# Staged weights, whole-slot splits, a rebuilt routing turn and a transposed large part in a two-layer mixture-of-experts kernel

## The chip, the cores and the metric

One NeuronCore of a Trainium2 chip runs the whole kernel in one launch. Its engines take their instructions in order, each from its own list: the tensor engine (PE, with its weight loads shown apart as PEld), the vector engine (DVE), the scalar engine (ACT), GpSimd (POOL) and SyncE (SP, which here only issues DMAs). The metric is the device time of one execution in microseconds (us), lower is better.

## The reference, cut to what matters

Three stages in a chain, on two batches of 576 tokens (1152 in all), width 512:

```python
# 1: linear attention, 8 heads a batch
q_p, k_p = phi(q), phi(k)             # [exp(p), exp(-p)] of p = x @ w_phi less its largest magnitude
out = (q_p @ (k_p.T @ v)) / (q_p @ k_p.sum() + 1e-6)
# 2: first mixture: every expert on every token, gates P made doubly stochastic in 8 rounds
for e in range(8):
    out += P[:, e:e+1] * (np.maximum(x @ w1[e], 0) @ w2[e])      # 512 -> 1024 -> 512
# 3: second mixture: each token at one expert, at most cap = 288 tokens each
logits = x @ w_gate; expert = argmax(logits); gate = softmax(logits)[expert]
pos = place of the token among those of its expert, in order of tokens
h = np.maximum(disp[e, pos] @ w1[e], 0); y = h @ w2[e]           # own weights, 8 experts
out[token] = gate * y    if pos < cap else 0
```

## The kernel before

All products are fp32 in effect: each operand is split as x = hi + lo, two numbers that PE takes at full rate, and a product is hi*hi + hi*lo + lo*hi.

The first mixture runs in 36 units (an expert's 256 features each); the tokens go in two groups. A unit's weights come by two DMAs of 512 KB (`r<-w1a`, `r<-w2a`, `Unit`, L190), ACT makes hi and POOL lo (`split1`, `split2`); layer 1 (L617 to 619) is seven products of blocks in place of eight, layer 2 (L670 to 672) goes to PSUM, and DVE adds it with its gate to `acc` (L681). Attention of the eight head pairs is interleaved with the first units by the framework's scheduler; the scheduler also places those DMAs in SP's list.

The turn between the mixtures is written by hand from `by_hand` (after L828) on. `Route` (L690) takes some of the nine tiles of 128 tokens through steps: `turn` transposes a tile of `acc`, `logits` multiplies by w_gate and takes the largest and its index, `pick` makes the one-hot `oh` and running counts `ohs`, `place` counts the tokens before each token of its expert (`cp`, in PSUM), `slots` makes the slot number, `gate` the gate, `scatter` writes rows with an indirect DMA to their slots in memory (`disp`). Tiles 0 to 3 (A) go early, 4 and 5 (B) next, 6 to 8 (C) last. For experts 0 and 1 the transposed rows of the first 64 slots are made on PE instead (`xst`): a product of the last five tiles with the selection matrix `sel` (L925), and of the rows that were scattered before with the identity (L931). `pair_split` makes hi and lo of them, and expert 0 begins.

The second mixture loops over the experts (L1205 on). The first 64 slots of an expert take the small path: `q1_small` (16 matmuls of 512 columns, hi and lo of x side by side), `gt_small` copies to SBUF, `ht_small` adds both halves and transposes, `relu_small` makes `hhl` (ACT the relu, DVE the lo, L1123), `q2_small` (16 matmuls), `out_small` adds the halves with the gate and writes rows with an indirect DMA. Slots 64 to 287 take `large`, under a branch on whether the expert has so many tokens; in the profiled execution experts 2 and 6 do. Each expert has 8 pieces of weights of 128x1024 (4 of w1b, 4 of w2b), loaded by SP into 4 KB slots (`load`), and split by `Splits`: ACT makes hi but of piece 4, which DVE makes; lo goes half a slot at a time (128x512, L571), of five pieces on DVE, of three on POOL, into another slot. The loop says which steps of the next expert stand where in the engines' lists.

Of the kernel before, what the change touches and what calls it, by code (L numbers as in the profile page):

```python
# [20 lines left out]
def tile_linear_attention_two_moe(  # L21
# [27 lines left out]
    # the first layer's tokens in groups, each of two halves  # L49
# [7 lines left out]
    # tiles of a batch's tokens; the last, a half, is of both heads of a pair, one above the other  # L57
# [43 lines left out]
    )  # L101
    twice = const.tile([P, 64], F32, name="twice")
# [29 lines left out]
    rings = {"a": ring, "b": ring, "x": ring}  # L132
# [14 lines left out]
    # x and its sums (A11, A21 + A22, .. of the seven products), hi and lo, by group and half of the chunks of a block  # L147
# [10 lines left out]
    # the first group's are in slots: the blocks that are made in pairs, and the single ones  # L158
# [31 lines left out]
    class Unit:  # L190
        """an expert's weights for FQ of its features: chunk 2 i + k of W1 is in half k of the rows"""
# [48 lines left out]
    def a_parts(i, key):  # L240
        """the first keys' first columns come by themselves"""
# [18 lines left out]
    def phi_group(hl, g, d, nm):  # L260
        """x w_phi - max|x w_phi| for one or two tiles of rows, both heads of the pair"""
# [101 lines left out]
    def a_xtrans(i, c):  # L363
# [8 lines left out]
        if len(full) < len(TGS[c]):  # L372
            # of a half tile's block, each head's rows have their own columns
# [23 lines left out]
    def x_sums(g, c):  # L397
        """the seven products' left sides; chunk 2 i + k of x is in half k of the columns"""
# [31 lines left out]
    lgs = {}  # L430
    # of each token: its expert, logits, logits less the largest, expert as a number, slot
# [3 lines left out]
    def gate_logits(g):  # L435
        """x w_gate; of the second half S1 = A21 + A22 by the first rows of w_gate, and A22 by what the others are more"""
# [49 lines left out]
    def zero_fill(what):  # L486
        """empty slots and zero rows, from a part of acc that nothing needs yet"""
# [17 lines left out]
    def take(key, shape, dt, name):  # L505
        """the slot that has been free for the longest"""
        at[key] = free.pop(0)
        return slot_at(at[key], shape, dt, name)

    def load(n, keep):  # L510
        """weights of the second layer's experts, in order: n pieces, but leave the slots for hi of keep's"""
        while n and todo:
            e, i = todo[0]
            if len(free) <= sum(x[0] <= keep and x not in sp.h for x in raws) + (e <= keep) + sp.more:
                break
            del todo[0]
            w, cc, W = (w1b, DC // 4, F) if i < 4 else (w2b, F // P // 4, D)
            raws[e, i] = take(("r", e, i), [P, cc, W], F32, f"rw_{e}_{i}")
            r0 = i % 4 * cc * P
            nc.sync.dma_start(raws[e, i], w[e, r0 : r0 + cc * P, :].rearrange("(c p) f -> p c f", p=P))  # L520
            n -= 1

    class Splits:
        """hi and lo of the second layer's weights, half a slot at a time; each engine takes its share in order"""

        WHOLE = "a"
        HI_V, LO_P, LO_P0, LATE = (4,), (0, 3, 5), (1, 2, 5), (4, 6, 7)

        def __init__(self):
            self.q = {k: [] for k in "avp"}  # L530
            self.spare, self.more = {k: [] for k in "vp"}, 2
            self.h, self.l, self.hi_todo, self.lo_todo = {}, {}, {}, {}
            for e in range(E):
                for i in range(8):
                    for k in range(2):
                        he = "v" if e and i in self.HI_V else "a"
                        le = "p" if i in (self.LO_P if e else self.LO_P0) else "v"
                        self.q[he].append(("hi", e, i, k))
                        self.q[le].append(("lo", e, i, k))
                        self.hi_todo[e, i, k], self.lo_todo[e, i, k] = he, le  # L540

        def emit(self, eng, most=2):
            what, e, i, k = self.q[eng].pop(0)
            r = raws[e, i]
            if (e, i) not in self.h:
                shape, nm = list(r.shape), f"h2_{e}_{i}"
                self.h[e, i] = take(("h", e, i), shape, R32, nm)
            n = 1
# [761 lines left out]
```

## Time and profile before

| | us |
|---|---|
| median of 3 runs (lowest, highest) | 1082.06 (1081.43, 1083.75) |
| profiled execution, span from first to last instruction | 1079.5 |
| PE busy | 1037.5 (96%) |
| DVE busy | 749.9 (69%) |
| POOL busy | 526.6 (49%) |
| ACT busy | 401.6 (37%) |
| HBM read, written | 84.25 MB, 11.51 MB |

Busy shares are means over the whole span; attention and the first mixture fill the first 894 us, the turn and the second mixture the rest, and these have different limits. The profile's views give: busy shares in 40 slices, groups of instructions by line and tile, the waits of an engine with what ended them, and the instructions in order of time.

### The profile page before, as it was taken

To read this page: it belongs to the slowest core of one execution; us is meant where nothing else is said; L and a number is where in the kernel's file an instruction comes from. 1 tells how busy PE (TensorE), PEld (TensorE's weight loads), DVE (VectorE), ACT (ScalarE), POOL (GpSimd) and SP (SyncE) were. 2 spreads that over 40 slices of the span, in tenths; PEclk is the share of its full clock that TensorE was granted. 3 is DMA by queue.
4 is the path that set the end of the run, shared out by engine and by line. 5 is a ranking of instruction groups with operands and counts; after the bars stand their busy time and mean duration, and the time that the engine had idled before them with its cause. 6 is when DMAs were issued, how large, how long until landed. Compare 5 with 4: busy or idle time off the path is not lost. (4 is left out here: it accounts for less than half of the span.)

```text
span 1079.5 us, 16720 instructions
## 1 busy us (share of the span) xinstructions
PE 1037.5 (96%) x6214; PEld 926.3 (86%) x6214; DVE 749.9 (69%) x1400; ACT 401.6 (37%) x841; POOL 526.6 (49%) x524
## 2 busy tenths in 40 slices
PE   7999999999999999999999999999999998798787
PEld 7999989898899899889988988898899888576566
DVE  6755799996666666666666666666667667946962
ACT  5767543322223222222232232223222235717532
POOL 4656897644454554444455544444542016625631
PEclk9999999999999999999999999999999998989889
DMA  8813132211112111111111111111111433967700
GB/s 272 273 53 89 62 98 79 79 59 40 39 40 59 49 51 39 39 40 39 46 53 59 40 40 40 39 41 59 58 57 63 131 110 104 323 229 239 264 7 25
DMA packets 56024, 95.21 MB, mean 88 GB/s; under 512 B 6206, under 2 KB 25022, under 8 KB 55936
## 3 DMA queue, kind: packets, MB, share of 16 engines
q1 hardware_dynamic: 54544, 91.41, 26.4%
q0 software_dynamic: 1392, 2.63, 0.7%
q8 instruction: 55, 0.90, 0.4%
q14 instruction: 33, 0.27, 0.1%
HBM read 84.25 MB, written 11.51 MB: 89 GB/s over the span
## 5 line engine op out<-in xcount | busy, mean ns | idle before, releaser
L81 POOL TENSOR_TENSOR l<-r,h 128x256 fp32r<-128x256 f32 (+2 forms) x100 | 154.2, 1555 | 351.4 <-ACT h L80 351.4
L681 DVE SCALAR_TENSOR_TENSOR acc<-p,prob,acc 128x512 f32<-128x512 f32 x252 | 188.3, 749 | 105.2 <-PE p L672 105.1
L670 PE MATMUL p<-h,hh 128*128 128x512 f32 x576 | 228.4, 396 | 0.0
L671 PE MATMUL p<-l,hh 128*128 128x512 f32 x576 | 227.4, 395 | 0.0
L672 PE MATMUL p<-h,hl 128*128 128x512 f32 x576 | 227.3, 395 | 0.0
L636 DVE TENSOR_TENSOR ca<-ca,p 128x256 f32<-128x256 f32 (+1 forms) x256 | 112.6, 449 | 70.2 <-PE p L619 68.0
L80 ACT CAST h<-r 128x256 fp32r<-128x256 f32 (+2 forms) x108 | 70.9, 686 | 184.8 <-PE p L672 163.6
L625 ACT ACTIVATE hh<-ca 128x320 fp32r<-128x320 f32 (+1 forms) x128 | 56.2, 442 | 217.9 <-DVE ca L636 217.9
L672 PEld LDWEIGHTS p<-h,hl 128*128 128x128 f32 x576 | 108.4, 188 | 25.6
L670 PEld LDWEIGHTS p<-h,hh 128*128 128x128 f32 x576 | 108.4, 188 | 22.4
L671 PEld LDWEIGHTS p<-l,hh 128*128 128x128 f32 x576 | 108.4, 188 | 22.3
L81 POOL TENSOR_TENSOR lt<-t,ht 128x256 fp32r<-128x256 f32 x144 | 124.9, 896 | 1.3 <-PE pn L349 1.3
L571 DVE TENSOR_TENSOR l<-rw,h 128x512 fp32r<-128x512 f32 x80 | 82.8, 1066 | 15.2 <-ACT h L558 13.3
L571 POOL TENSOR_TENSOR l<-rw,h 128x512 fp32r<-128x512 f32 x48 | 69.7, 1474 | 30.1 <-ACT h L558 23.2
L617 PE MATMUL p<-xh,ht 128*128 128x320 f32 x256 | 79.2, 309 | 0.0
L619 PE MATMUL p<-xh,lt 128*128 128x320 f32 x256 | 79.1, 309 | 0.0
L618 PE MATMUL p<-xl,ht 128*128 128x320 f32 x256 | 79.1, 309 | 0.0
L617 PE MATMUL p<-xs,ht 128*128 128x256 f32 x256 | 72.9, 285 | 0.7 <-DVE cb L636 0.5
L619 PE MATMUL p<-xs,lt 128*128 128x256 f32 x256 | 72.6, 284 | 0.0
L618 PE MATMUL p<-xs,ht 128*128 128x256 f32 x256 | 72.4, 283 | 0.0
L636 DVE TENSOR_TENSOR cb<-cb,p 128x320 f32<-128x320 f32 (+1 forms) x128 | 58.0, 453 | 19.0 <-PE p L619 18.0
L629 DVE SCALAR_TENSOR_TENSOR hl<-ca,hh 128x320 fp32r<-128x320 f32 (+1 forms) x128 | 65.7, 515 | 2.5 <-ACT hh L625 2.0
(253 smaller groups left out, 2296.6 us busy)
## 6 DMA issues: line engine op xcount, KB each, us to landing
r<-w1a SPq DMA_DIRECT2D x36, 512.0 KB, 3.5
r<-w2a SPq DMA_DIRECT2D x36, 512.0 KB, 3.8
rw<-w1b SPq DMA_DIRECT2D x32, 512.0 KB, 6.1
rw<-w2b SPq DMA_DIRECT2D x32, 512.0 KB, 8.4
disp<-acc SPq DMA_DIRECT2D x18, 260.0 KB, 4.9
v<-va SPq DMA_DIRECT2D x8, 325.0 KB, 3.7
rawq<-qT SPq DMA_DIRECT2D x8, 320.0 KB, 4.7
out<-acc SPq DMA_DIRECT2D x9, 256.0 KB, 5.5
```

Source lines behind the costliest of these rows:

```text
L80: nc.scalar.copy(hi, src)
L81: (eng or nc.vector).tensor_tensor(lo, src, hi, ALU.subtract)
L571: en.tensor_tensor(self.l[e, i].rearrange("p c f -> p (c f)")[:, ks], rv, hv, ALU.subtract)
L617: nc.tensor.matmul(ps, ws_[0], xs[0], start=i == 0, stop=False)
L618: nc.tensor.matmul(ps, ws_[0], xs[1], start=False, stop=False)
L619: nc.tensor.matmul(ps, ws_[1], xs[0], start=False, stop=i == DI - 1)
L629: nc.vector.scalar_tensor_tensor(lv[:, qs], src, 0.0, hv[:, qs], ALU.max, ALU.subtract)
L636: nc.vector.tensor_tensor(o, x, ps, ALU.add)
L670: nc.tensor.matmul(ps, a, w.w2[0][:, f, :], start=f == 0, stop=False)
L671: nc.tensor.matmul(ps, a, w.w2[1][:, f, :], start=False, stop=False)
L672: nc.tensor.matmul(ps, b_, w.w2[0][:, f, :], start=False, stop=f == FT - 1)
L681: nc.vector.scalar_tensor_tensor(o, ps, prob[:, t, e : e + 1], o, ALU.mult, ALU.add)
```

## The change

- `stage`: after each layer 2 of a unit two pieces of the second mixture's weights are copied in memory, from w1b and w2b to `wst`, where a piece is 128 rows of 4 KB; `load` reads `wst`. Three more slots "f" and one more "e".
- `Splits`: ACT makes all hi, lo is made in whole slots in the place of the raw weights: expert 0's on POOL during the last units, all others on DVE.
- `Route`: B is tiles 4 and 5, C 6 and 7, Z 8; `place` adds -4096 in PSUM where a token is at an expert, and `select` compares `cp` with numbers that carry the same mark; slots and gates of tiles 4 to 8 are made together (R); exponentials come from PSUM with the largest as bias; one scatter of five tiles at the end.
- The loop: lo of the next expert's pieces and all hi at new places; the rest of the steps inside the branch, between the features of `large`, or in its other arm; loads eight before and four after the slots come free.
- `large`: weights are the stationary side, 224 tokens the moving one; h comes out transposed.
- `dynamic_dma_scratch_size=4096`.

```diff
+    def stage(n):
+        for e, i in staged[:n]:
+            src = piece(e, i)
+            nc.sync.dma_start(wst[e, i].rearrange("p (c f) -> p c f", c=src.shape[1]), src)
+        del staged[:n]
...
-            nc.sync.dma_start(raws[e, i], w[e, r0 : r0 + cc * P, :].rearrange("(c p) f -> p c f", p=P))
+            nc.sync.dma_start(raws[e, i], wst[e, i].rearrange("p (c f) -> p c f", c=src.shape[1]))
...
-        HI_V, LO_P, LO_P0, LATE = (4,), (0, 3, 5), (1, 2, 5), (4, 6, 7)
+                    le = "v" if e else "p"
+            h, l = self.h[n], r.bitcast(R32)
+            self.put(eng, lambda: en.tensor_tensor(l, r, h, ALU.subtract))
...
+        def aside(self, hi, lo):
+            steps = {k: [] for k in "avp"}
+            self.put, put = (lambda eng, f: steps[eng].append(f)), self.put
+            self.run("v", -1, lo)
+            self.run("a", -1, hi)
...
+                todo = before[::-1] + [(tri_b, oh[:, t, :]), (far_b, oh[:, t, :])]
...
+        def select(self, iota_s):
+                nc.vector.tensor_tensor(
+                    sel[:, j], iota_s, self.cp[:, j * E : j * E + EP].unsqueeze(2).to_broadcast([P, EP, C0]), ALU.is_equal
+                )
...
                 if pend:
                     yield from layer2(*pend)
+                    stage(2)
...
+                        sp.run("p", 6, (0, 7))
...
-        A, B, C = (Route(range(*r)) for r in ((0, 4), (4, 6), (6, NT)))
+        A, B, C, Z = (Route(range(*r)) for r in ((0, 4), (4, NT - 3), (NT - 3, NT - 1), (NT - 1, NT)))
+        R = Route(range(4, NT))
...
+        Z.place()
+        Z.exps(0)
+        sp.run("a", 4, (1, 7))
+        C.select(iota_s)
+        Z.select(iota_s)
...
+        R.slots()
+        R.gate()
+        rows_of([xs0], [ident])
+        rows_of([acc[:, Z.t0]], [Z.sel[:, 0]], last=True)
+        xhl = pair_split(0, xqp, xst)
+        R.scatter()
...
+        def q1(f):
+            for c in range(DC):
+                nc.tensor.matmul(ps, w1[0][c][:, fs], xh[:, c], start=c == 0, stop=False)
+                nc.tensor.matmul(ps, w1[0][c][:, fs], xl[:, c], start=False, stop=False)
+                nc.tensor.matmul(ps, w1[1][c][:, fs], xh[:, c], start=False, stop=c == DC - 1)
+            nc.scalar.activation(hh, ps, AF.Relu)
+            nc.vector.scalar_tensor_tensor(hl, ps, 0.0, hh, ALU.max, ALU.subtract)
+            for k in "av":
+                if aside[k]:
+                    aside[k].pop(0)()
+        def q2(f):
+            for i, (_, n) in enumerate(chunks):
+                nc.tensor.matmul(o, hh[:, ts], w2[0][f], start=f == 0, stop=False)
+                nc.tensor.matmul(o, hh[:, ts], w2[1][f], start=False, stop=False)
+                nc.tensor.matmul(o, hl[:, ts], w2[0][f], start=False, stop=f == F // P - 1)
...
-        sp.run("a", 2, nx)
+        sp.run("v", 8, (e + 1, AHEAD - 1))
...
+        sp.run("a", 8, (e + 1, AHEAD + 1))
...
+        aside = sp.aside((e + 2, AHEAD + 1), (e + 2, AHEAD - 1))
...
+            with more.Else():
+                for f in aside["a"] + aside["v"]:
+                    f()
+        load(8, E)
         sp.done(e)
-        load(4, e + 2)
+        load(4, E)
```

DVE's list where expert 3's small path stands, from the branch of expert 2 to the output of expert 2. `rw` is a raw piece, `h` its hi, `l` its lo, `hhl` the relu's lo, `y` the output. Before:

```order
L1245 UNCONDITIONAL_BRANCH x2
L558 CAST h_3_4_10684<-rw_4_10083 128x512
L571 TENSOR_TENSOR l_3_4_10686<-rw_4_10083,h_3_4_10684 128x512
L558 CAST h_3_4_10684<-rw_4_10083 128x512
L571 TENSOR_TENSOR l_3_4_10686<-rw_4_10083,h_3_4_10684 128x512
L571 TENSOR_TENSOR l_3_6_10692<-rw_6_10087,h_3_6_10690 128x512 x2
L571 TENSOR_TENSOR l_3_7_10697<-rw_7_10089,h_3_7_10695 128x512 x2
L1123 SCALAR_TENSOR_TENSOR hhl_0_10756<-ht_0_10751,hhl_0_10756 128x4x64
L1123 SCALAR_TENSOR_TENSOR hhl_1_10766<-ht_1_10761,hhl_1_10766 128x4x64
L81 TENSOR_TENSOR xhl_10769<-xst_10744,xhl_10769 128x8x64
L1138 SCALAR_TENSOR_TENSOR y_10775<-q_2_10461,tails_9745,y_10775 64x512
```

The same place of the change, with the arm of expert 2 that runs when it has few tokens:

```order
L572 TENSOR_TENSOR rw_5_10524<-rw_5_10524,h_3_5_10579 128x1024
L572 TENSOR_TENSOR rw_6_10526<-rw_6_10526,h_3_6_10604 128x1024
L572 TENSOR_TENSOR rw_7_10528<-rw_7_10528,h_3_7_10605 128x1024
L572 TENSOR_TENSOR rw_0_10530<-rw_0_10530,h_4_0_10606 128x1024
L572 TENSOR_TENSOR rw_1_10532<-rw_1_10532,h_4_1_10607 128x1024
L572 TENSOR_TENSOR rw_2_10534<-rw_2_10534,h_4_2_10608 128x1024
L1235 UNCONDITIONAL_BRANCH
L572 TENSOR_TENSOR rw_3_10861<-rw_3_10861,h_4_3_10886 128x1024
L1130 SCALAR_TENSOR_TENSOR hhl_0_10912<-ht_0_10907,hhl_0_10912 128x4x64
L1130 SCALAR_TENSOR_TENSOR hhl_1_10920<-ht_1_10915,hhl_1_10920 128x4x64
L81 TENSOR_TENSOR xhl_10927<-xst_10900,xhl_10927 128x8x64
L1145 SCALAR_TENSOR_TENSOR y_10933<-q_2_10587,tails_9822,y_10933 64x512
```

The steps ahead of hhl are whole slots now, and of the expert after next.

PE's list at the end of the turn: `xst` are the transposed rows, `xs` the rows scattered before, `q` the second layer's first product. Before:

```order
L931 MATMUL xst_0_9645<-ident,xs_9259 128x128
L931 MATMUL xst_1_9646<-ident,xs_9259 128x128
L931 MATMUL xst_2_9647<-ident,xs_9259 128x128
L931 MATMUL xst_3_9648<-ident,xs_9259 128x128
L936 LDWEIGHTS ones_b
L936 MATMUL pcn<-ohs,ones_b 1x8
L925 MATMUL xst_0_9645<-sel_9674,acc 128x128 x3
L925 MATMUL xst_1_9646<-sel_9674,acc 128x128 x3
L925 MATMUL xst_2_9647<-sel_9674,acc 128x128 x3
L925 MATMUL xst_3_9648<-sel_9674,acc 128x128 x3
L1103 MATMUL q_0_0_9772<-h_0_0_9190,xhl_9711 128x512
```

The same place of the change:

```order
L916 MATMUL xst_0_9649<-sel_9674,acc 128x128 x2
L916 MATMUL xst_1_9650<-sel_9674,acc 128x128 x2
L916 MATMUL xst_0_9649<-sel_9738,acc 128x128 x4
L916 MATMUL xst_1_9650<-sel_9738,acc 128x128 x4
L949 LDWEIGHTS ones_b
L949 MATMUL pcn<-ohs,ones_b 1x8
L916 MATMUL xst_0_9649<-ident,xs_9332 128x128 x2
L916 MATMUL xst_1_9650<-ident,xs_9332 128x128 x2
L916 MATMUL xst_0_9649<-sel_9741,acc 128x128 x2
L916 MATMUL xst_1_9650<-sel_9741,acc 128x128 x2
L1110 MATMUL q_0_0_9838<-h_0_0_9091,xhl_9777 128x512
```

The products of three tiles that stood last are now those of one, and the other tiles' products stand ahead of the rows from memory; all of these stand behind the last tile's placement.

SP's list between the loads of attention's last pairs and of units 1 and 2 (`rawq`, `v` of attention; `r_1`, `r_2` a unit's weights). Before:

```order
L249 DMA rawq_1095<-qT 128x640
L251 DMA v_928<-va 128x650
L251 DMA v_1097<-va 128x650
L198 DMA r_2_1551<-w1a 128x4x256
L200 DMA r_2_1553<-w2a 128x2x512
L198 DMA r_1_1547<-w1a 128x4x256
```

The same place of the change:

```order
L254 DMA rawq_1098<-qT 128x640
L528 DMA wst<-w2b 256x1x512 x4
L256 DMA v_931<-va 128x650
L528 DMA wst<-w1b 16x8192 x4
L528 DMA wst<-w2b 256x1x512 x2
L256 DMA v_1100<-va 128x650
L203 DMA r_2_1554<-w1a 128x4x256
L205 DMA r_2_1556<-w2a 128x2x512
L528 DMA wst<-w2b 256x1x512 x2
L528 DMA wst<-w1b 16x8192 x4
L528 DMA wst<-w2b 256x1x512
L203 DMA r_1_1550<-w1a 128x4x256
```

The copies stand between the loads; four more stand ahead of this piece, the rest up to the load of unit 11.

## Rows read from the trace of the kernel before

**Rows 1.** The page: busy tenths of PE and its granted clock, 40 slices

```profile
PE   7999999999999999999999999999999998798787
PEclk9999999999999999999999999999999998989889
```

**Rows 2.** Timeline of PE in the turn: start, us, engine, line, operation, [idle before]

```profile
896.01 0.17 PE L750 MATMUL cp<-oh,tri_b 128*128 128x8 bf16 x1 [1.69 <-DVE oh L735]
...
902.36 3.76 PE L925 MATMUL xst<-sel,acc 128*128 128x128 f32 x16
...
907.97 2.94 PE L925 MATMUL xst<-sel,acc 128*128 128x128 f32 x24
910.67 0.48 PE L1103 MATMUL q<-h,xhl 128*128 128x512 f32 x1
```

**Rows 3.** Timeline of PE: first and last matmul of expert 7

```profile
1064.11 0.39 PE L1103 MATMUL q<-h,xhl 128*128 128x512 f32 x1
...
1073.40 0.39 PE L1131 MATMUL q<-l,hhl 128*128 128x512 f32 x1
```

**Rows 4.** Waits of PE, 911 to 1079.5: us in total, times, longest

```profile
PE q L1130 <- DVE hhl L1123: 21.9, 6, 5.4
```

**Rows 5.** Timeline of DVE, part of expert 4

```profile
997.71 3.46 DVE L571 TENSOR_TENSOR l<-rw,h 128x512 fp32r<-128x512 f32 x5
1001.09 0.75 DVE L1123 SCALAR_TENSOR_TENSOR hhl<-ht,hhl 128x256 fp32r<-128x256 f32 x2
1001.76 0.73 DVE L1138 SCALAR_TENSOR_TENSOR y<-q,tails,y 64x512 f32<-64x512 f32 x1
1002.41 6.24 DVE L571 TENSOR_TENSOR l<-rw,h 128x512 fp32r<-128x512 f32 x4
```

**Rows 6.** Timeline of POOL, the same time

```profile
1003.89 9.04 POOL L571 TENSOR_TENSOR l<-rw,h 128x512 fp32r<-128x512 f32 x6
```

**Rows 7.** Timeline of PE, large part of expert 2, to expert 3's first matmul

```profile
952.51 0.93 PE L1146 MATMUL xst<-ident,xs 128*128 128x128 f32 x8
...
955.80 1.09 PE L1162 MATMUL q<-h,x_0l 128*128 128x512 f32 x4
...
977.77 0.39 PE L1103 MATMUL q<-h,xhl 128*128 128x512 f32 x1
```

**Rows 8.** Groups of ACT, 911 to 1079.5: busy us, mean ns, idle before

```profile
L558 ACT CAST h<-rw 128x1024 fp32r<-128x1024 f32 x40 | 40.4, 1045 | 11.0 <-issue 6.1 <-POOL l L571 2.3 <-PEq L1245 2.0
L1109 ACT COPY gt<-q 128x512 f32<-128x512 f32 x16 | 9.4, 584 | 9.3 <-PE q L1104 7.1 <-DVEq L1245 1.2 <-DVE h L558 1.1
L1137 ACT ACTIVATE y<-q,tails 64x512 f32<-64x512 f32 x8 | 5.5, 684 | 3.3 <-PE q L1131 2.9 <-DMA tails<-disp 0.2
```

**Rows 9.** Windows: us, busy of PE, PEld, DVE, ACT, POOL, clock, DMA share, GB/s

```profile
36.00:41.00 5.00, 5.00 (x46) 5.00 (x46) 2.79 (x10) 3.83 (x11) 5.00 (x7) 1.00 0.96 328
840.00:880.00 40.00, 40.00 (x239) 35.85 (x239) 24.87 (x53) 8.88 (x15) 4.95 (x3) 1.00 0.39 132
```

**Rows 10.** Timeline of PE: two matmuls of 256 columns, attention

```profile
61.21 0.28 PE L270 MATMUL pjq<-wbd_h,hhkq 128*128 128x256 f32 x1
61.33 0.28 PE L271 MATMUL pjq<-wbd_l,hhkq 128*128 128x256 f32 x1
```

**Rows 11.** Timeline of DVE in the turn

```profile
892.73 3.23 DVE L735 TENSOR_TENSOR oh<-iota_e,rt_e 128x16 bf16<-128x16 f32 x1
```

**Rows 12.** Timeline of POOL in the turn

```profile
893.40 2.51 POOL L571 TENSOR_TENSOR l<-rw,h 128x512 fp32r<-128x512 f32 x2
```

**Rows 13.** Timeline of SP: loads of units 1 and 11

```profile
103.00 0.37 SPq L198 DMA_DIRECT2D r<-w1a  x1
...
208.39 0.37 SPq L198 DMA_DIRECT2D r<-w1a  x1
```

**Rows 14.** Timeline of POOL: unit 6's last splits

```profile
155.60 3.46 POOL L81 TENSOR_TENSOR lt<-t,ht 128x256 fp32r<-128x256 f32 x4
```

**Rows 15.** Timeline of PE: unit 6's first matmul

```profile
185.32 0.31 PE L617 MATMUL p<-xh,h 128*128 128x320 f32 x1
```

More of the change, by code (lines that the diff above doesn't have):

```diff
@@ L508, in take, with piece @@
         return slot_at(at[key], shape, dt, name)
+    staged = [(e, i) for e in range(E) for i in range(8)]
+    wst = dram.tile([E, 8, P, 4 * P * DC // 2], F32, name="wst")
+    def piece(e, i):
+        w, cc = (w1b, DC // 4) if i < 4 else (w2b, F // P // 4)
+        r0 = i % 4 * cc * P
+        return w[e, r0 : r0 + cc * P, :].rearrange("(c p) f -> p c f", p=P)
+    def stage(n):
[3 more added lines that the diff above has]
+        del staged[:n]
     def load(n, keep):
@@ L513, in load @@
             e, i = todo[0]
-            if len(free) <= sum(x[0] <= keep and x not in sp.h for x in raws) + (e <= keep) + sp.more:
+            if len(free) <= sum(x[0] <= keep and x not in sp.h for x in raws) + (e <= keep):
                 break
             del todo[0]
-            w, cc, W = (w1b, DC // 4, F) if i < 4 else (w2b, F // P // 4, D)
-            raws[e, i] = take(("r", e, i), [P, cc, W], F32, f"rw_{e}_{i}")
-            r0 = i % 4 * cc * P
-            nc.sync.dma_start(raws[e, i], w[e, r0 : r0 + cc * P, :].rearrange("(c p) f -> p c f", p=P))
+            src = piece(e, i)
@@ L533, in __init__ @@
+            self.put = lambda eng, f: f()
             for e in range(E):
                 for i in range(8):
[L535 to L540, printed above, removed]
@@ L593, in need @@
+        def aside(self, hi, lo):
[3 more added lines that the diff above has]
+            self.run("a", -1, hi)
+            self.put = put
+            return steps
         def need(self, e, iis):
             for i in iis:
-                for k in range(2):
-                    for todo in (self.hi_todo, self.lo_todo):
-                        while (e, i, k) in todo:
-                            self.emit(todo[e, i, k])
+                while (e, i) in self.lo_todo:
+                    self.emit(self.lo_todo[e, i])
@@ L835, in moe1_run @@
         h = yield from layer1(u, 0, w)
-        sp.need(0, range(2))
         free.extend(f"x{n}" for n in range(7))
-        load(7, -1)
+        sp.run("p", 8, (0, 7))
+        load(8, 1)
         yield from layer2(*pend)
@@ L859, in moe1_run @@
         A.logits(1)
+        A.exps(0)
         next(l1)
+        A.exps(1)
         next(l1)
         A.logits(2)
-        A.rest()
-        next(l1)
-        next(l1)
         A.turn(3)
         next(l1)
-        A.pick(0, 3)
+        A.exps(2)
+        next(l1)
+        A.logits(3)
+        next(l1)
+        A.pick()
+        A.count()
+        A.exps(3)
         next(l1)
@@ L875, in moe1_run @@
         free.extend(f"c{n}" for n in range(8))
-        A.logits(3)
-        A.pick(3)
+        load(8, 1)
         l2 = layer2(u, 1, w, h)
-        load(2, 0)
+        A.place()
         next(l1, None)
         next(l2)
-        A.place()
-        sp.run("a", 2, 0)
-        A.exps()
+        A.own()
         A.slots()
@@ new lines, in moe1_run, with rows_of @@
+        B.exps(1)
+        xst = [bank(f"xst_0_{k}")[:, : 2 * P] for k in range(2)]
+        def rows_of(ts, sels, first=False, last=False):
+            for k in range(2):
+                for x, sel in zip(ts, sels):
+                    for c in range(2):
+                        nc.tensor.matmul(
+                            xst[k][:, c * P : (c + 1) * P], x[:, (2 * k + c) * P : (2 * k + c + 1) * P], sel,
+                            start=first and c == 0, stop=last, skip_group_check=True,
+                        )
@@ L929, in rows_before @@
-        def rows_before(cs):
-            for c in cs:
-                nc.tensor.matmul(xst[c], xs0[:, c * P : (c + 1) * P], ident, start=False, stop=False)
-        rows_of(B)
-        C.place()
-        rows_before(range(DC))
+        B.own()
+        C.pick()
+        C.count(0, 1)
+        Z.logits(0)
+        rows_of([acc[:, B.t0]], [B.sel[:, 0]], first=True)
+        C.place()
+        for j in range(C.n):
+            C.exps(j)
+        Z.pick()
+        Z.place()
+        Z.exps(0)
+        sp.run("a", 4, (1, 7))
@@ L936, in moe1_run @@
+        C.select(iota_s)
+        Z.select(iota_s)
+        rows_of([acc[:, B.t0 + 1]], [B.sel[:, 1]])
+        rows_of([acc[:, t] for t in C.ts], [C.sel[:, j] for j in range(C.n)])
+        C.own()
+        Z.own()
+        C.count(1)
+        Z.count()
+        R.slots()
+        R.gate()
         nc.tensor.matmul(pcn[0:1, 0:E], ones_b[:, 0:1], ohs[:, NT - 1, :], start=True, stop=True)
-        C.slots(iota_s)
-        C.exps()
-        C.gate()
-        C.scatter()
+        rows_of([xs0], [ident])
```

294 lines of the change are left out of this document (107 added, 187 removed).

## The prediction

> **What bounds the kernel now.** I read the slices of the span first: the tensor engine (PE) is full from the second slice to the 33rd and has holes in the last seven, where the granted clock also falls between its two levels [rows 1]. So the first 890 us are PE-bound; an edit there can only cost time, and the change has to earn what it earns between the last first-layer matmul and the end. The timeline gives that part's two pieces. The last second matmul of the first layer ends at 896.01 - 1.69 = 894.3, the second layer begins at 910.67 [rows 2]: the turn, 16.4 us. The second layer's last matmul ends at 1073.8 [rows 3]: 163.1 us.
>
> Within the second layer the waits of PE have one large entry: 21.9 us in six waits for hhl, a short operation on the vector engine (DVE) [rows 4]. It is short itself (0.38 us) but stands behind the splits of the next expert's weights on an engine that takes its instructions in order. The DVE rows of one expert show why the queue is long [rows 5]: five lo steps take 3.46 us, 0.69 each, when POOL is not splitting; four take 6.24, 1.56 each, while POOL's own six run from 1003.89 for 9.04 us [rows 6]. The two engines slow each other by more than a factor of two; the splits that POOL takes off DVE cost DVE most of what they save. Without the two large parts of 25.3 us [rows 7] and expert 7 the second layer is 163.1 - 50.6 - 9.7 = 102.8, 14.7 us for each of the other seven small parts; PE alone needs 1073.8 - 1064.1 = 9.7 us for expert 7, which waits for nothing [rows 3].
>
> **Splits and order in the second layer.** Removed: POOL's three pieces per expert, DVE's hi of piece 4. Added to DVE: eight lo of 128x1024 for every expert from 1 on, each one instruction in the place of two. Before shows no 128x1024 subtraction on DVE. Bounds: twice 0.69 = 1.38 above; below, 1.05, the ACT copy of that size [rows 8]. I take 1.2, since one of two fixed parts goes. DVE then has 8 x 1.2 + 0.75 + 0.73 = 11.1 us for an expert, against 3.46 + 0.75 + 0.73 + 6.24 = 11.2 before, with two hi and a lo of piece 4 on top of these rows [rows 5]. ACT has 8 x 1.05 + 2 x 0.58 + 0.68 = 10.2 [rows 8] and two relus about as long as DVE's hhl, 0.8: 11.0. Loads: a stretch of stores moved 328 GB/s at a share of 0.96 [rows 9], so 512 KB cost 1.53 us and eight cost 12.3; but 23 of 64 pieces are issued before expert 0 branches, so the queue doesn't set the pace. DVE and ACT are nearly equal now and both stand close to PE's 9.7.
>
> The order of the steps decides what shows. hi steps of experts 1 and 2 stand in the branch behind q2_small and thus ahead of gt in ACT's queue, and seven lo steps plus one stand ahead of hhl on DVE. Following these queues by hand with the prices above gives, from one expert's first matmul to the next: 10.4 (expert 0, splits from the turn), 12.0, 12.7, 10.2 (its splits were done during expert 2's large part), 14.6, 11.4, 13.4, 9.6. Sum 94.3.
>
> **The large part**, run for experts 2 and 6. Before: transposes from 952.51, next expert from 977.77: 25.3 us [rows 7]. Four 512-column matmuls take 1.09 with 0.39 for the last one's own length, so a step is 0.233. q1 now is 96 matmuls of 224 columns. Nothing of that width is in the trace; a 256-column step is 0.12 [rows 10], in proportion to its columns 0.105, so I take 0.116. Sum: entry 1.6 (transposes 0.93 [rows 7], the rest a split), 96 x 0.116 = 11.1, q2 48 x 0.233 = 11.2, end 0.3: 24.2 each. The 16 transposes of h that fall away are what the longer entry and q1's extra steps do not eat. ACT has a relu and a hi per f, about 1.4 us, and DVE 1.6, beside PE's 2.8, so the steps put in between are free.
>
> Second layer: 94.3 + 48.4 = 142.7, less 163.1: **-20.4**. Bounds: if PE waited for nothing, 10.4 + 7 x 9.7 + 48.4 = 126.7 (-36); if lo costs 1.38 and six experts take 15 each, 10.4 + 90 + 9.6 + 48.4 = 158.4 (-5).
>
> **The turn.** The one-hot of tiles 4 and 5 took 3.23 us for 16 columns (hhl takes 0.38 for 256), with POOL splitting beside it [rows 11, 12]; PE waited 1.69 for it [rows 2]. With POOL done before (e0's eight lo, about 8 x 3.0 = 24 us, fall where POOL is busy only 4.95 of 40 us [rows 9]) that wait goes, and the six-step slot chain no longer stands ahead of the selection. What is late next is the transposed rows: 24 f32 products of two records each, before and after alike; 16 records took 3.76 at the low clock and 24 took 2.94 [rows 2]. Earlier all of the last three tiles' 24 came after the last selection, now 8 do, but 32 more wait behind Z's placement, which needs the last tile's sum, transposes, logits and maximum. Before, PE is through with that tile's logits at 902.36, 8.0 us after 894.3 [rows 2]; without the wait of 1.69, and with the other tiles' logits done ahead of the last sum, I estimate 4.8 with the placement. Then 40 records at 0.123 to 0.235 are 4.9 to 9.4, and the split 0.8: the second layer begins 10.5 to 15.0 us after 894.3 in place of 16.4. I take 12.4: **-4.0**, bounds -6 and -1.4. DVE's slot and gate steps, 14 short ones, stand ahead of the split's lo but beside those products. The five scatters come after it; expert 1's end needs their rows.
>
> **Staging.** 64 copies of 512 KB from memory to memory enter SP's queue, between the loads of attention and of units 1 to 11: 21 ahead of r_1, issued at 103.00, the other 43 ahead of r_11, at 208.39 [rows 13]. PE is full there, so a late weight costs its whole lateness beyond the slack. The slack: unit 6's last lo ends at 155.60 + 3.46 = 159.1 [rows 14] and PE begins the unit at 185.32 [rows 15]: 26.3 us. Before shows no such copy. If it costs what a store costs, 1.53, the 43 copies and 18 loads take 93 of 105.4 us: hidden, cost 0. The queue stays ahead as long as 43c + 18 x 1.53 is under 105.4 + 26.3, up to c = 2.4 us. If the copy's read and write count apart, c = 3.06, the loads come 27 us too late. I take 0: the nearest row is the one of stores, and that a copy costs no more than a store of its size is my assumption. The Trainium skill, HBM Reference, Specifications, gives a core some 358 GB/s of its memory; if reading and writing shared that, a copy would cost an estimated 2.9 us and all of the gain but a little would be gone. The same page says that a core alone measures more, limited by its DMA engines; no run here shows a copy. In return the weights of w2 are read in 4 KB rows in place of 2 KB; since loads run ahead, I count 0 for it.
>
> **Sum.** The profiled execution's span is 1079.5; the median of the runs is 1082.06, 2.6 more. 1079.5 - 20.4 - 4.0 = 1055.1, plus 2.6: **1057.7**.
>
> **Rivals.**
> 1. *The wait for hhl stays* (chance 0.20). A hi that waits for its load, or gt behind eight hi, delays relu and hhl; DVE and ACT become a chain instead of running side by side. For: both queues are in order and 11 to 13 instructions long; DVE's 11.1 and ACT's 11.0 leave little. Against: no POOL beside them. Gains of 5 to 12 in the second layer and 2 to 4 in the turn: 1066 to 1076.
> 2. *PE becomes the bound everywhere* (0.12). For: DVE's 1.05 end of the bound gives 9.9 us for an expert, about PE's 9.7. Then 126.7 to 132: 1041 to 1049.
> 3. *The copies delay the first layer* (0.13): slower than before. Place: SP's queue before r_1 to r_11; price 27.4 us at c = 3.06; together 1057.7 + 27.4 = 1085. It cancels the gain from c = 3.0 on; between 2.4 and 3.0 part of the gain stays (1060 to 1080). For: 34 MB to read and 34 MB to write before 208 us, and v of pairs 5 to 7 is in the same queue. Against: at a store's price they fit, with 12 us to spare besides the slack.
> 4. *The scatters stall* (0.05): five indirect stores of 266 KB are issued in a row with a smaller space for their descriptors. If each must land before the next is written, 4 x 0.8 us by the rate of [rows 9] and the way of each come on top, and the rows of expert 2's pair are late by some 5 us: 1063.
>
> **How the numbers follow.** Forecast as worked out, within 1049 to 1066: 0.50. With the rivals the range from 1044 to 1077 leaves out about a third of rival 2 and most of the slow end of rivals 1 and 3, under 2 in 10. A measurement of this kernel tells changes over 0.2% (2.2 us) from none. Slower: rival 3 beyond c = 3.0, 0.09, and mishaps like it, 0.01; same: 0.03; faster: 0.87.
>
> **What would show it.** In the profile after: lo 128x1024 on DVE at 1.2 us without POOL beside it; PE's wait for hhl under 8 us in all; large(2) at 24 us; the first q1 matmul 12 to 13 us after the last matmul of the first layer; unit 6 begun at 185 as now. Wrong would be: a unit begun later than before by more than 2 us (copies), lo above 1.4, ACT's gt later than PE's q1 by more than 3 us in several experts, or a second layer of more than 150 us.

## The result and the profile after

The changed kernel takes 1052.39 us, median of 4 runs (1049.29 to 1054.03), beside 1081.74 for the kernel before in the same comparison (4 runs, 1079.12 to 1083.75): ratio 0.9725, 95% interval 0.9695 to 0.9756. Forecast were 1057.7, within 1044 to 1077. The profiled execution has a span of 1049.5 us, 30.0 less than before. All that follows is an account of these 30.0.

The page's slices after, which answer to [rows 1]: the granted clock is at nine tenths or more up to the 37th slice, before up to the 33rd, and PE's last slices are fuller (one of 7 tenths where there were three).

```profile
PE   8999999999999999999999999999999999889887
PEclk9999999999999999999999999999999999999899
```

The timeline of PE at the turn (start, us, engine, line, operation), for [rows 2]:

```profile
888.77 0.39 PE L669 MATMUL p<-h,hl 128*128 128x512 f32 x1
...
892.62 1.81 PE L916 MATMUL xst<-sel,acc 128*128 128x128 f32 x8
...
894.60 3.74 PE L916 MATMUL xst<-sel,acc 128*128 128x128 f32 x24
...
898.36 1.16 PE L916 MATMUL xst<-ident,xs 128*128 128x128 f32 x8
899.35 1.06 PE L916 MATMUL xst<-sel,acc 128*128 128x128 f32 x8
900.88 0.50 PE L1110 MATMUL q<-h,xhl 128*128 128x512 f32 x1 [0.47 <-DVE xhl L81]
...
1043.33 0.39 PE L1138 MATMUL q<-rw,hhl 128*128 128x512 f32 x1
```

The first layer ends at 888.77 + 0.39 = 889.16, before at 894.33: **-5.2**, which the prediction had at nothing. The turn is 900.88 - 889.16 = 11.72 in place of 16.34: **-4.6** (forecast -4.0). The second layer ends at 1043.72 and lasts 142.84 in place of 163.12: **-20.3** (forecast -20.4). Together -30.1; the ends differ by the last 0.1.

PE's waits in the second layer, which answer to [rows 4] (us in total, times, longest):

```profile
PE q L1137 <- DVE hhl L1130: 5.1, 4, 1.8
PE q L1110 <- PEq L1235: 4.2, 3, 2.3
PE ht L1122 <- ACT gt L1116: 2.0, 2, 1.7
PE xst L1157 <- DMA xs<-disp: 0.7, 2, 0.4
```

Two of these entries were small before:

```profile
PE q L1103 <- PEq L1245: 0.9, 3, 0.3
PE ht L1115 <- ACT gt L1109: 0.3, 1, 0.3
```

The 21.9 us for hhl have become 5.1; the wait at the branch of an expert, in PE's own sequencer, has grown from 0.9 to 4.2, and that for gt from 0.3 to 2.0. DVE's rows beside them, for [rows 5], and the groups of lo and hi, for [rows 8]:

```profile
971.13 9.15 DVE L572 TENSOR_TENSOR rw<-rw,h 128x1024 fp32r<-128x1024 f32 x8
980.21 0.74 DVE L1130 SCALAR_TENSOR_TENSOR hhl<-ht,hhl 128x256 fp32r<-128x256 f32 x2
982.43 0.74 DVE L1145 SCALAR_TENSOR_TENSOR y<-q,tails,y 64x512 f32<-64x512 f32 x1 [1.49 <-ACT y L1144]
```

```profile
L572 DVE TENSOR_TENSOR rw<-rw,h 128x1024 fp32r<-128x1024 f32 x56 | 65.0, 1214 | 4.3 <-ACT h L564 4.3
L564 ACT CAST h<-rw 128x1024 fp32r<-128x1024 f32 x52 | 51.0, 1044 | 0.1
```

Eight lo take 9.15 us, 1.14 each in a row and 1.21 as the group's mean: the 1.2 of the forecast. DVE does not run without a gap: it waits 1.49 for y, since ACT has two hi of 1.04 ahead of it (e9 is on that).

The view of windows separates PE's waiting from its working over the second layer (stretch, length, busy time of PE, PEld, DVE, ACT and POOL, granted clock, DMA share, GB/s), first before, then after:

```profile
910.67:1073.79 163.12, 137.09 (x639) 108.09 (x637) 112.95 (x130) 81.16 (x121) 73.07 (x53) 0.92 0.56 184
```

```profile
900.88:1043.72 142.84, 128.99 (x700) 106.44 (x700) 86.59 (x107) 81.41 (x118) 34.95 (x14) 0.96 0.48 176
```

PE's idle time falls from 26.0 to 13.9 (-12.2), its busy time from 137.1 to 129.0 (-8.1). Of the second, the two large parts are about 3 (e11). Most of the rest goes with a granted clock of 0.96 in place of 0.92: of the 256 products of 512 columns in the small parts, 40 took over 0.55 us before and 16 do after, and such products start some 0.44 us apart in place of 0.23, which makes an estimated 5 us.

### The profile page after: what moved, and what is told of

Same layout as the page of the kernel before. It is cut to its first block, busy times and chain, and to the rows that moved or that the text cites. A ratio compares the mean times of both kernels' runs of the same rounds, so it can differ in the third digit from the quotient of the medians.

```text
span 1049.5 us, 16803 instructions
## 1 busy us (share of the span) xinstructions
PE 1021.6 (97%) x6294; PEld 922.0 (88%) x6294; DVE 719.2 (69%) x1352; ACT 406.7 (39%) x853; POOL 498.4 (47%) x484
## 5 line engine op out<-in xcount | busy, mean ns | idle before, releaser
L667 PEld LDWEIGHTS p<-h,hh 128*128 128x128 f32 x576 | 108.3, 188 | 20.4
L626 DVE SCALAR_TENSOR_TENSOR hl<-ca,hh 128x320 fp32r<-128x320 f32 (+1 forms) x128 | 68.7, 538 | 2.1 <-ACT hh L622 1.4
L572 DVE TENSOR_TENSOR rw<-rw,h 128x1024 fp32r<-128x1024 f32 x56 | 65.0, 1214 | 4.3 <-ACT h L564 4.3
L564 ACT CAST h<-rw 128x1024 fp32r<-128x1024 f32 x64 | 62.9, 1044 | 6.7 <-PE p L668 4.3
```

The source lines that it names most:

```text
L572: self.put(eng, lambda: en.tensor_tensor(l, r, h, ALU.subtract))
L626: nc.vector.scalar_tensor_tensor(lv[:, qs], src, 0.0, hv[:, qs], ALU.max, ALU.subtract)
L667: nc.tensor.matmul(ps, a, w.w2[0][:, f, :], start=f == 0, stop=False)
```

## The experiments

Times are medians, ratios to the kernel before on the same chip.

**e1: place of two tiles.** The first layer gained 5.2 us though no instruction of it changed.

```diff
+    pad_a = xp.tile([P, 64], F32, name="pad_a")
     twice = const.tile([P, 64], F32, name="twice")
...
     slot_i = xp.tile([P, NT], I32, name="slot_i")
+    pad_b = xp.tile([P, 16], F32, name="pad_b")
```

> The kernel before with two unused tiles of 256 and 64 bytes a partition, which move every later tile of the left side of SBUF by 256 to 320 bytes, as the change's new small tiles do. The change made the first layer end 5.2 us earlier, 0.1 us for every second product of a unit, in lines that it does not touch (mean step of a matmul of layer 2 0.2329 before, 0.2289 after). Theory A: the step depends on where its tiles lie; expected 1077, with the first layer's end at 889 and a step near 0.229. Rival B: it comes from the smaller descriptor space or from anything else in the change; expected 1082, step 0.233.

1074.64 us, ratio 0.9934 (0.9916 to 0.9952): nothing but unused bytes makes the old kernel 0.7% faster. This view of one line (last product of a feature in the first layer; count, ns min/median/max, first and last start) shows it for the last 485 products of the line; before, after, and e1:

```profile
L672 PE MATMUL p<-h,hl x485: 390/393/404, 255.8 to 893.9; 128*128 128x512 f32 x162
```

```profile
L669 PE MATMUL p<-h,hl x485: 388/394/398, 256.2 to 888.8; 128*128 128x512 f32 x162
```

```profile
L674 PE MATMUL p<-h,hl x485: 388/394/398, 255.4 to 888.1; 128*128 128x512 f32 x162
```

The same products take 638.1, 632.6 and 632.7 us. Each lasts as long as ever; the distance between starts is less, 0.2327 us before and 0.2291 after and in e1. This is the mean over neighbouring products of the three lines of the first layer's second half, from 256 to 880 us, without the breaks over 0.3.

**e2: the smaller space for descriptors alone.**

```diff
-    nc = bacc.Bacc("TRN2", target_bir_lowering=False, num_devices=1)
+    nc = bacc.Bacc("TRN2", target_bir_lowering=False, num_devices=1, dynamic_dma_scratch_size=4096)
```

> The kernel before with the descriptor space at 4096 alone, which moves the left side's tiles by 12288 bytes. Theory A (place within some hundred bytes): no change, 1082, step 0.233. Rival B (the space itself, or the place in thousands of bytes): 1077, first layer's end 5 us earlier. For the scatters: if the smaller space makes an indirect store wait for one that has not drained, some of the stores on POOL last 4 us and more in place of 1, here too, and the end does not move, since rows are needed late.

1080.99 us, ratio 1.000 (0.9988 to 1.0012). The indirect stores take 0.90 to 1.16 us, as before, so the smaller space alone makes none of them long. In the changed kernel some are:

```profile
901.40 0.97 POOL L787 DMA_INDIRECT disp<-acc,slot_i  x1 [0.30 <-issue]
902.68 4.67 POOL L787 DMA_INDIRECT disp<-acc,slot_i  x1 [0.31 <-issue]
...
971.48 9.59 POOL L1099 DMA_INDIRECT out<-y,tails  x1 [7.87 <-DVE y L1145]
```

The one of 9.59 begins 0.35 us into DVE's run of eight whole-slot lo, shown above at 971.13, and ends 0.8 after the last of them. The one of 4.67 begins 0.80 into a run of four. In e5 it is the fourth of the five that takes 5.05 and the fifth 0.98: there a run of four begins 0.41 before the fourth. In e9 the store that took 9.59 is issued just before the run, and it is short:

```profile
970.18 0.92 POOL L1101 DMA_INDIRECT out<-y,tails  x1 [5.97 <-DVE y L1147]
```

```profile
970.30 9.18 DVE L574 TENSOR_TENSOR rw<-rw,h 128x1024 fp32r<-128x1024 f32 x8 [0.39 <-ACT h L566]
```

So a store is long where it begins within a run of whole-slot lo, and not where it follows other stores, as rival 4 had it. In runs of two whole slots stores take 1.7, beside runs of halves 1.1 to 1.2 (e4). Whether whole slots do this with the larger space as well was not run.

**e3: the copies alone.** The kernel before, with the 64 copies after the same units and its loads reading wst.

```diff
-            nc.sync.dma_start(raws[e, i], w[e, r0 : r0 + cc * P, :].rearrange("(c p) f -> p c f", p=P))
+            nc.sync.dma_start(raws[e, i], wst[e, i].rearrange("p (c f) -> p c f", c=cc))
...
                     yield from layer2(*pend)
+                    stage(2)
```

> The kernel before with the 64 copies and with the weights of the second mixture loaded from them, nothing else. Theory: the copies are hidden and the loads ran ahead anyway: 1082 within 2. Rival: loads of 4 KB rows are what shortened the second layer: 1072 to 1078, with expert 5's and 6's waits for hhl shorter. Other rival: copies late for units 1 to 11: 1085 and more.

1081.2 us, ratio 0.9995 (0.9983 to 1.0007): no loss, no gain. The load of unit 11 goes out at 208.85 and unit 6 begins at 184.90, before 208.39 and 185.32 [rows 13, 15]. The windows from the load of unit 1 to that of unit 11, before and e3:

```profile
103.00:209.00 106.00, 105.09 (x677) 94.44 (x677) 93.12 (x198) 49.25 (x121) 84.48 (x93) 1.00 0.28 85
```

```profile
103.00:209.00 106.00, 104.86 (x677) 94.36 (x676) 93.23 (x197) 48.91 (x120) 84.24 (x93) 1.00 0.85 291
```

The share of the DMA engines rises by 0.57 of 106 us for about 42 copies: 1.44 us of the engines' time each, against the 1.53 taken from the row of stores.

**e4: POOL's three lo to DVE.** The kernel before with one entry of its table emptied.

```diff
-        HI_V, LO_P, LO_P0, LATE = (4,), (0, 3, 5), (1, 2, 5), (4, 6, 7)
+        HI_V, LO_P, LO_P0, LATE = (4,), (), (1, 2, 5), (4, 6, 7)
```

> The kernel before with POOL's three lo pieces of experts 1 to 7 given to DVE (16 halves on DVE in place of 10), in halves as before. Theory (the two engines slow each other by the whole of what POOL takes over): DVE per small expert 16 x 0.69 + 2 x 0.42 + 1.5 = 13.4 in place of 15.6, so 6 experts gain about 2 us each: 1068 to 1074. Rival (POOL's share really relieves DVE): 6 halves more, 4 us for each of 6 experts: 1100 to 1106.

1067.25 us, ratio 0.9876 (0.9852 to 0.9900): a little more than expected. The second layer takes 151.4 us in place of 163.1, the -12 of the theory; in this profile the first layer also ends 1.8 earlier, which the edit does not touch. More work on the engine that PE waits for makes PE wait less:

```profile
PE q L1130 <- DVE hhl L1123: 11.5, 5, 3.3
```

```profile
980.33 5.32 DVE L571 TENSOR_TENSOR l<-rw,h 128x512 fp32r<-128x512 f32 x8
```

Eight lo of 512 take 5.32 us, 0.67 each, where four took 6.24 beside POOL [rows 5]. PE's idle time in the second layer falls from 26.0 to 151.4 - 136.7 = 14.7, nearly the 13.9 of the changed kernel. This one part of the change, on the kernel before, thus gives nearly all of the shorter waits; whole slots, in place, save further DVE time (86.6 busy against 101.6) that PE no longer waits for.

**e5 to e8: which place counts.** The changed kernel with unused bytes at the left, where the first layer's relu hh (the stationary operand) lies, or at the right, where its split weights (the moving one) lie: 64 bytes left (e5, the first line below), 32 left (e6), 32 right (e7, the second line), 32 on both sides (e8). A pad moves the later tiles of its side too, not these alone.

```diff
+    pad_l = xp.tile([P, 16], F32, name="pad_l")
...
+    pad_r = ctx.enter_context(pool("padr", side="right")).tile([P, 8], F32, name="pad_r")
```

> The changed kernel with 64 unused bytes more on the left side: the stationary tiles of layer 2 lie at 96 of each 128 bytes again, as in the kernel before, the moving ones (slots) stay at 96. Theory A1 (a step is longer where both operands have the same place in 128 bytes): step 0.233 again, 1057. Theory A2 (only the place in 64 bytes counts, 32 for all of them in both kernels): nothing moves, step 0.2296, 1052; the step would then hang on something coarser than 128 bytes.

> The changed kernel with 32 bytes more on the left: the stationary tiles and the results of DVE and ACT lie at 64-byte places, the slots at 32 of 64. A1: residues differ (64 and 96), step 0.2296 or a little less, 1052. A2: step shorter, 0.225, 1044.

> The changed kernel with 32 bytes on the right: the slots (moving tiles of layer 2 and of the second mixture, stationary ones of layer 1) lie at 64-byte places, the left side stays at 32 of 64. A1: residues 32 and 64 differ, 1052. A2: moving reads at 64-byte places are shorter: step 0.225 or less in layer 2, 1040 to 1046; no effect on 0.133 in layer 1, whose moving tiles are partly on the left.

> The changed kernel with 32 bytes on either side: all these tiles at 64 of 128 bytes. A1: the same residue for both, step 0.233, 1057. A2: everything at a 64-byte place, shortest steps of the four, 1036 to 1045.

| | us | ratio (95%) | last 485 products of the line, us | step, us | stationary - moving, bytes mod 512 |
|---|---|---|---|---|---|
| before | 1081.7 | | 638.1 | 0.2327 | 128 |
| after | 1052.4 | 0.9725 (0.9695 to 0.9756) | 632.6 | 0.2291 | 448 |
| e1 | 1074.6 | 0.9934 (0.9916 to 0.9952) | 632.7 | 0.2291 | 448 |
| e5 | 1050.6 | 0.9711 (0.9683 to 0.9739) | 630.5 | 0.2277 | 0 |
| e6 | 1059.9 | 0.9797 (0.9748 to 0.9846) | 638.2 | 0.2333 | 480 |
| e7 | 1059.5 | 0.9794 (0.9748 to 0.9840) | 638.2 | 0.2333 | 480 |
| e8 | 1054.6 | 0.9748 (0.9720 to 0.9776) | 630.5 | 0.2277 | 0 |

Both theories on record fall: neither tile's own address orders the four runs. What does is the distance of the two tiles, from the addresses in the built programs: 0 is fast, then 448, and 480 and 128 are slow. e5 and e8 have the same distance at different places, and so have e6 and e7. In e2 the left side lies 12288 bytes lower, 24 times 512, and the step is the 0.2327 of the kernel before; that 512 is the period is not shown by this. The rule was found after the runs, over four distances, so e12 tests it.

**e9: ACT's order.** e5 with ACT's hi moved behind y and xhl.

```diff
         hs.append(relu_small(e, 1, ht))
-        sp.run("a", 8, (e + 1, AHEAD + 1))
...
             out_small(e - 1, done)
+        sp.run("a", 8, (e + 1, AHEAD + 1))
         done = q2_small(e, hs, w2)
```

> The changed kernel with the 64 bytes of e5_l64 and one step moved: the two hi casts of the second expert ahead, which stand on ScalarE before this expert's output and the split of the next expert's rows, are issued behind both, just before q2. Theory (ScalarE's order sets the 5.4 us that PE waits for hhl, since DVE's lo steps stand behind an xhl or y that waits for two hi of 1.0 us): DVE's waits for ScalarE's xhl and y go from 1 to 2 us to under 0.5 us, PE's wait for hhl falls to under 2 us, and the run takes 1043 to 1047 us against e5's 1050.6. Rival (DVE's eight lo are as long as PE's expert, so that the order moves the wait and does not shorten it; or the hi come late and lo waits for them): hhl or a rw wait of the same 4 to 6 us stays, 1049 to 1052 us. Slower than 1052 would show that gt waits behind the hi moved towards it.

1049.29 us, 5 runs, ratio 0.9695 (0.9673 to 0.9717), the fastest of all, but its interval overlaps those of e5 and of the changed kernel. PE's waits:

```profile
PE q L1112 <- PEq L1237: 5.7, 4, 3.4
PE xst L1159 <- DMA xs<-disp: 3.6, 2, 3.2
PE ht L1124 <- ACT gt L1118: 3.2, 3, 1.8
PE q L1139 <- DVE hhl L1132: 1.0, 3, 0.5
```

The theory is right on its place (hhl 5.4 in e5, now 1.0) and wrong on its worth: at the branches, for expert 2's rows and for gt PE waits 12.5, where it waited 2.1 + 0.7 + 2.3 = 5.1 in e5. PE's idle time is 144.6 - 129.7 = 15.0 beside e5's 146.4 - 132.4 = 14.0. The gain of 1.3 in the median is no more than the lower busy time of a clock of 0.96 against 0.94 would give; no gain of the order is shown.

**e10: POOL busy through the turn.**

```diff
         A.scatter()
+        for _ in range(12):
+            nc.gpsimd.tensor_tensor(busy, busy, busy, ALU.subtract)
```

> The changed kernel with GpSimd kept busy through the turn: twelve subtractions of 128x192 on a tile that nothing else reads are issued on it behind the first scatters, from about 889 us on. Theory (the wait of 1.69 us for the one-hot before came from GpSimd working beside DVE, and the rebuilt turn gains because GpSimd is idle there): DVE's two-input steps of the turn (selection 0.23 each, one-hot 0.17, counts 0.18) take twice as long or more, and the time from the last first-layer matmul to the first q1 matmul grows from 11.7 to 13.2 to 16 us; total 1053 to 1057. Rival (the turn is bound by TensorE's products and the order alone): 11.7 to 12.3 us, total within 1 us of the changed kernel (1052.4).

1050.98 us (2 runs, 1047.67 and 1054.30), ratio 0.9716 (0.9675 to 0.9756). Some of DVE's steps take about twice as long, two of the one-hots (0.35 and 0.42 for 0.17) and one pair of counts (0.75 for 0.36); another count (0.16) and the selections (0.47 for two, as after) do not:

```profile
890.87 0.75 DVE L736 TENSOR_TENSOR ohs<-ohs,oh 128x8 bf16<-128x8 bf16 x2
...
893.65 0.47 DVE L753 TENSOR_TENSOR sel<-iota_s,cp 128x128 f32<-128x128 f32 x2
...
895.25 0.35 DVE L725 TENSOR_TENSOR oh<-iota_e,rt 128x16 bf16<-128x16 f32 x1
```

PE has no wait for them. But this is not the load of the kernel before. There POOL had two lo of 128x512 in a row, 2.51 us, and the step of DVE beside them took 3.23 [rows 11, 12]; here POOL's subtractions take 0.58 each, and they begin at 891.53, behind the one-hot of tiles 4 and 5. In e1, which has the turn of the kernel before, that one-hot takes 0.17, the counts behind it are the long step, and it is these that PE waits for:

```profile
887.08 3.27 DVE L747 TENSOR_TENSOR ohs<-ohs,oh 128x8 bf16<-128x8 bf16 x2
```

```profile
887.60 2.51 POOL L573 TENSOR_TENSOR l<-rw,h 128x512 fp32r<-128x512 f32 x2
```

```profile
890.20 0.17 PE L756 MATMUL cp<-ohs,ones_b 128*128 128x8 bf16 x1 [1.67 <-DVE ohs L747]
```

In all six profiles with the old turn (before, e1 to e4, e11) one step of DVE is long, 3.0 to 3.2 us, and ends within 0.05 of POOL's second lo, whichever step it is: the one-hot in four, the counts in e1 and e11. In the changed kernel the counts end 1.9 us before PE takes them (888.38 and 890.25); three us more would show as a wait of an estimated 1.1. So e10 does not test what made the wait before, and e1 speaks for the theory's reason.

The turn is 13.35 us here, in the range that the theory gave, but not by its reason. The windows of the turn say why; before, after, e10 and e5:

```profile
894.33:910.67 16.34, 13.75 (x88) 13.40 (x87) 10.93 (x52) 6.68 (x13) 9.58 (x9) 0.69 0.29 97
```

```profile
889.16:900.88 11.72, 11.25 (x101) 10.86 (x99) 5.75 (x34) 7.01 (x15) 2.71 (x3) 0.85 0.77 269
```

```profile
892.01:905.36 13.35, 12.88 (x102) 12.48 (x100) 6.20 (x34) 7.01 (x15) 9.20 (x16) 0.74 0.69 248
```

```profile
886.09:896.31 10.22, 9.75 (x102) 9.41 (x100) 5.78 (x34) 7.01 (x15) 1.95 (x2) 1.00 0.78 273
```

PE idles 0.47 in each of the last three and 2.59 before (1.69 for the one-hot, 0.91 for the last sum); the rest is the granted clock, 0.69, 0.85, 0.74 and 1.00, over nearly the same products (24 rows' records take 3.74 after, 4.91 in e10, 2.92 in e5; busy time times clock is 9.5, 9.6, 9.5 and 9.8). So the turn's -4.6 are 2.1 of waits and 2.5 of busy time, which follows the clock. Whether POOL's work had to do with the clock in e10 isn't settled by one profile.

**e11: the large part alone.** The kernel before with the new form of `large`, without steps put in between, and with one more PSUM bank for this part and one less for the others.

```diff
-                nc.tensor.matmul(ps, xx_[i][0][:, c], w1[0][c][:, fs], start=c == 0, stop=False)
...
-                nc.tensor.transpose(ps[:, c * P : c * P + n], gts[i][f][:n, c * P : (c + 1) * P], ident[:n, :n])
...
+                nc.tensor.matmul(ps, w1[0][c][:, fs], xh[:, c], start=c == 0, stop=False)
+            nc.scalar.activation(hh, ps, AF.Relu)
+            nc.vector.scalar_tensor_tensor(hl, ps, 0.0, hh, ALU.max, ALU.subtract)
```

> The kernel before with one thing of the change: its large part has the new form (all rows at once, q1 of 224 columns with the weights held still, relu and hi per f, no transposes of h), without steps of the next expert put in between; the tiles of 512 columns that only the old form used are gone. Theory (the large part costs 24.0 us in place of 25.3 because the 16 transposes of h go): large(2) and large(6) take 24.0 to 24.6 us each from their transposes to the next expert's first matmul and the run takes 1078.5 to 1080.5 us against 1081.5. Rival (what the large part gains is given back, since the next expert's splits still set when that expert can go on): large parts of 24, and the experts behind them longer by as much, 1081 to 1082. As the tiles that go change addresses, a first-layer step other than 0.2334 us is taken apart from this: only the second layer counts for the two theories.

1078.04 us (10 runs), ratio 0.9972 (0.9958 to 0.9987): -3.2. From the transposes to the next expert's first product:

```profile
954.89 0.94 PE L1147 MATMUL xst<-ident,xs 128*128 128x128 f32 x8
...
978.61 0.40 PE L1100 MATMUL q<-h,xhl 128*128 128x512 f32 x1
```

23.7 us, and the second one from 1040.12 to 1063.82 as long, where it was 25.3 and 25.2, a little below the theory's 24.0. The second layer takes 160.4 us in place of 163.1, -2.7, so at most 0.4 of these 3.1 is given back. In the changed kernel the large parts are 24.3 and 23.7.

**e12: the old place in the new kernel.** e5's pad made 192 bytes, which puts the two tiles where they were before, modulo 512.

```diff
+    pad_l = xp.tile([P, 48], F32, name="pad_l")
```

> The changed kernel with 192 unused bytes in the place of e5's 64: hh and the split weights of the first layer then lie at the same addresses, modulo 512 bytes, as in the kernel before (96 and 480). Theory (the place of these two tiles alone sets the step of the first layer's second matmuls; nothing else of the change does): the step is 0.2325 to 0.2345 us as before, in place of 0.2285 to 0.23, the last first-layer matmul ends at 893 to 896 us, the second layer stays at 141 to 146 us, and the run takes 1055 to 1060 us. Rival (something else of the change shortens the step, such as the routing steps placed between the matmuls or the smaller space for descriptors): the step stays at 0.2285 to 0.23, the end of the first layer at 886 to 890, and the run takes 1049 to 1053 us.

1057.53 us, ratio 0.9794 (0.9772 to 0.9816), and the line's view as before the change:

```profile
L671 PE MATMUL p<-h,hl x485: 390/393/404, 255.9 to 893.9; 128*128 128x512 f32 x162
```

638.0 us, as before (638.1). The step is 0.2327 again, as the theory had it. Everything else of the change is there and the first layer's gain is gone, so the place makes it. That it is the place of these two tiles is argued from the lines whose step moves, since the pad moves the later tiles of the left side too. The kernel now takes 1057.53, where 1057.7 was forecast; its turn is 10.23 us at a clock of 1.00, its second layer 146.2 at 0.94. Why the distance matters is not known from these runs.

## Why the prediction was right, step by step

- **What bounds the kernel.** Right: PE up to the turn, then DVE's queue with POOL beside it. e4 shows the pair directly, 0.67 against 1.56 us a lo, and is worth 11.7 of the 20.3 by itself.
- **Second layer, -20.4 for -20.3.** The sum is better than its parts, and its agreement to 0.1 is luck. From one expert's first product to the next: forecast 10.4, 12.0, 12.7, 10.2, 14.6, 11.4, 13.4, 9.6; measured 11.6, 10.9, 13.3, 10.3, 15.5, 12.4, 11.2, 9.6 (sum 94.8 for 94.3), and the large parts 24.3 and 23.7 for 24.2 each. The order of the queues does decide where it waits: expert 4 is the longest, as worked out. The waits at branches (1.64 after expert 0, 2.25 after expert 5) stood in no term; expert 6 came out 2.2 shorter. Nor had it that 8.1 of the 20.3 are busy time of PE, with the clock in it: the same second layer took 141.4 us at a clock of 0.98 (e10) and 149.0 at 0.94 (e6), with 2.5 us more of waits in e6.
- **lo of 128x1024, 1.2 us.** 1.21.
- **Turn, -4.0 for -4.6.** PE's wait for the one-hot went, as worked out, and 0.91 for the last sum with it; the other half was the clock, which the text had only as the two prices of a record. That POOL's rest is what took the wait away is borne out by e1, where the long step and the wait move with POOL's two lo; e10 does not test it. The turn's size is partly luck: 11.7 us is just under the 12 to 13 that were to show it, and the same turn took 10.2 at a clock of 1.00 (e5, e12), under the lower bound of 10.5, and 13.4 at 0.74 (e10).
- **Staging, 0.** Shown by e3, on the margin too: 1.44 us a copy, under the 2.4 from which it would have cost. If the 358 GB/s that the Trainium skill (HBM Reference, Specifications) gives a core were shared by reading and writing, a copy would have cost an estimated 2.9. The run disagrees with that reading: with each copy counted at both ends, the 30.99 MB moved from 103 to 209 us in the changed kernel and the 22.0 MB of its 42 copies are 53 MB in 106 us, 500 GB/s. The other sentence of the Trainium skill there, that a core alone measures more, agrees in direction.
- **The rivals.** The wait for hhl stayed only at 5.1 (rival 1); PE did not become the only bound, with 13.9 us of waits (rival 2); no unit came late from the copies (rival 3: unit 11's load went out at 209.22, 0.8 later, and unit 6 began at 185.77, 0.45 later; in e3, with the copies alone, it began 0.42 earlier, so the copies are not shown to do this). Rival 4's stall, each store waiting for the one before, did not show: in e10 all five stores in a row take 0.97 to 0.99, and the long ones, of 4.67 and 9.6 us, go with DVE's runs of whole-slot lo (e2). PE's waits for rows are 0.7 us in all. By its own terms rival 1 ends at 1075 and not 1076.
- **What failed: "the first 890 us are PE-bound; an edit there can only cost time".** A PE-bound stretch still has a rate, and 5.2 us, which stood in no term, came from tiles that moved by some bytes: for the forecast this was luck, and it is nearly all of what 1057.7 lacks to 1052.4. With the tiles put back (e12) the time is 1057.53 and the ratio 0.9794, where 1057.7 is 0.9775 of 1082.06: a miss of 0.2 to 2 us, partly by misses that cancel, for the turn is 2.2 shorter there than forecast and the second layer 3.5 longer.

## What to carry to other kernels

When a helper engine shares work with the engine that the bound one waits for, time its instructions with and without the helper before counting on it: here four subtractions beside POOL cost more than eight without. Split a stage into busy and idle time of the bound engine together with its clock before crediting an edit, for both move. And when a stage gains or loses without an edit to its instructions, put the tiles back with unused bytes: 32 bytes were worth 5.6 us of the first layer here (e6, e7), more than the new large part.

## What the runs showed of the hardware

- The distance between the starts of 512-column fp32 products changed with the place of the two operands, from 0.2277 us (distance 0 modulo 512 bytes) over 0.2291 (448) to 0.2327 (128) and 0.2333 (480), with the time of one unchanged at 0.39.
- In the changed kernel PE waits 1.64 and 2.25 us at two of its branches and 0.30 at another; before, three waits of 0.30. In e9 the instruction queue moved a packet at 996.0 to 996.5, while PE stood at a branch from 995.6 to 999.0; that code came late is not shown by this.
- An indirect store that begins within a run of four or eight subtractions of 128x1024 on DVE lasts until 0.8 to 0.9 us after the last of them: 4.67 and twice 9.6 us in the changed kernel, in a run of two 1.7, against 0.90 to 0.98 outside such runs; just before a run it takes 0.92 (e9). The smaller space alone changed nothing (e2).
- A short step of DVE beside two lo of 128x512 on POOL (2.51 us) ended within 0.05 us of the second: 3.0 to 3.2 us in place of 0.17, a one-hot in the kernel before, a count in e1.
